# Where eleven weight conversions stand among the first chunk's products

## The chip, the core and the metric

The kernel runs on one core of a Trainium2 chip. The metric is the device time of one execution in microseconds. The time before is 731.13 us, the median of three runs (729.48 to 731.27). A difference under 0.3%, about 2.2 us, is taken as no change.

## The reference

Three stages follow each other. Stage one is attention on inputs of shape (4, 8, 768, 64), with a local window, a few global columns and a distance bias. Stage two is a feed-forward layer on the 3072 rows that come out, and it is the stage that the change touches. Stage three is a soft mixture of eight experts.

```python
def _moe_ref(x, w_in, w_out) -> np.ndarray:
    h = x @ w_in
    g = h * (1.0 / (1.0 + np.exp(-h)))
    return (g @ w_out).astype(np.float32)
```

Here x has 3072 rows of 512, w_in is 512 by 2048 and w_out 2048 by 512. NumPy draws both weights in float64, so each number reaches the chip as a pair of 32-bit words.

## The kernel before

The 3072 rows are 24 tiles of 128, in eight chunks of three. For each chunk the first layer runs 16 steps (`l1_step`, f = 0 to 15): twelve products of 128 by 384 on TensorE into one of four banks in turn (lines 502 to 504), a tanh on ScalarE (506), a gate on VectorE (508) and a split of the result into a float16 high part (ScalarE, 199) and low part (VectorE, 209). Then the second layer (`l2_part`, lines 522 to 524) sums over the same 16 blocks. The attention of the next chunk's tiles is cut into items that are dealt out after each step by `slot_end`: scores on TensorE (315 or 325), bias and maximum on VectorE (330), exponentials on ScalarE (331), splits (199, 201, 207, 209), transposes by DMA (348, 393), and products with the values (370).

Each weight is cut into eight pieces: 0 to 7 of w_in, 8 to 15 of w_out. Piece p of w_in serves first-layer steps 2p and 2p+1; piece 8+p of w_out serves second-layer blocks 2p and 2p+1. `w_ahead` loads a piece (1 MB, line 450, on SyncE's queue) into one of six staging places as soon as that is free, and `conv(p)` turns it into two float16 parts:

- line 460, ScalarE, and 462, VectorE: pick out exponent bits and mark bits;
- line 467, TensorE: two small products that gather the mark bits; after every odd piece 469, ScalarE, reads their bank before the next piece may write it;
- line 470, VectorE: join the words to a float32, over the bits that 467 read;
- line 480, ScalarE: the high part; 488, VectorE: the low part. This frees the staging place.

Pieces 8 to 15 reuse places 4, 5 and 3: piece 9 goes where piece 5 was, 10 where 3 was, then 11 where 8 was, 12 where 9 was, 13 where 10 was, 14 where 11 was, 15 where 12 was.

Pieces 0 to 4 are converted during the first chunk's attention (`START`), and the change leaves them alone. The loop of the first chunk calls `conv` for 5, 6 and 7 in front of steps 10, 12 and 14, and for 8 to 15 in front of the second layer's pairs of blocks. A scheduler then turns the program into a fixed order per engine, in which independent instructions may move forward; each engine runs its own list in order. In that list the first instructions of a conversion (460, 462) already stand early, the later ones (467 to 488) near the place of the call.

Of the kernel before, what the change touches and what calls it, by code (L numbers as in the profile page):

```python
# [45 lines left out]
def p2(e):  # L46
    return float(2.0 ** e)
# [33 lines left out]


START = [3, 9, 14, 18, 22, 99, 99, 99]
HE = 'AAAAAA'
PHE = 'AAAAAA'
PLE = 'VVVVVV'
# [13 lines left out]
def fast_kernel(tc, keepp, q_l, k_l, v_l, q_f, k_f, n_global, n_local, w_in, w_out, phi, w1, w2, shapes, pick_c, out):  # L100
# [8 lines left out]
    with ExitStack() as ctx:  # L109
# [160 lines left out]
        def split(T):  # L270
            t, u = T % TPB, T % NR
            he = HE[T] if T < len(HE) else "P"
            le = HLO[T] if T < len(HLO) else "V"
# [172 lines left out]
        def w_ahead():  # L446
            while nload[0] < 16 and holder.get(place[nload[0]]) is None and (GATE.get(nload[0]) is None or GATE[nload[0]] in done_p):
                p = nload[0]
                holder[place[p]] = p
                nc.sync.dma_start(out=ar.view(place[p], [2048], I32), in_=(w_in if p < 8 else w_out)[p % 8].bitcast(I32))  # L450
                nload[0] += 1

        def conv(p):
            assert holder[place[p]] == p
            st = ar.view(place[p], [1024, 2], I32)
            low, high = st[:, :, 0], st[:, :, 1]
            by = ar.view(place[p], [2048], I32).bitcast(U8).rearrange("p (n e) -> p n e", e=8)
            u16 = ar.view(place[p], [2048], I32).bitcast(U16).rearrange("p (n e) -> p n e", e=4)

            A.activation(out=low, in_=by[:, :, 3], func=AF.Copy, scale=1.0 / 32, bias=-0.484375)  # L460

            V.tensor_scalar(out=u16[:, :, 1], in0=u16[:, :, 3], scalar1=0xF000, scalar2=0x3000, op0=ALU.bitwise_and, op1=ALU.bitwise_xor)

            zb = u16[:, :, 1].bitcast(BF16)
            for j in range(2):
                g = 32 * (2 * (p % 2) + j)
                mm(bM[g:g + 32], wz, zb[:, 512 * j:512 * j + 512], start=True, stop=True, tile_position=(0, g))
            if p % 2 == 1:
                A.activation(out=odd16, in_=bM, func=AF.Abs, accum_out=oddp[:, p // 2:p // 2 + 1])
            V.scalar_tensor_tensor(out=low, in0=high, scalar=3, in1=low, op0=ALU.logical_shift_left, op1=ALU.bitwise_xor)  # L470
            lowf = ar.view(place[p], [1024, 2], F32)[:, :, 0]
            if p < 8:
                dst = [wih[:, z, :, 256 * p:256 * p + 256] for z in range(2)]
                src = lowf.rearrange("p (k f) -> p k f", k=4)
                e = E_WI
            else:
                dst = [woh[:, 2 * (p - 8):2 * (p - 8) + 2, z] for z in range(2)]
                src = lowf.rearrange("p (k f) -> p k f", k=2)
                e = E_WO
            A.activation(out=dst[0], in_=src, func=AF.Copy, scale=-p2(e - 128))  # L480
            if LOE[p] != "V":
                if LOE[p] == "P":
                    A.activation(out=src, in_=src, func=AF.Copy, scale=-p2(e - 128))
                else:
                    G.tensor_scalar(out=src, in0=src, scalar1=-p2(e - 128), scalar2=0.0, op0=ALU.mult, op1=ALU.add)
                G.tensor_tensor(out=dst[1], in0=src, in1=dst[0], op=ALU.subtract)
            else:
                V.scalar_tensor_tensor(out=dst[1], in0=src, scalar=-p2(e - 128), in1=dst[0], op0=ALU.mult, op1=ALU.subtract)  # L488
            holder[place[p]] = None
            w_ahead()  # L490
# [330 lines left out]
        nconv = 0  # L821
        before = START
        for i, it in enumerate(first_items()):
# [6 lines left out]
        for c in range(NCH):  # L830
            todo = items[upto[c]:upto[c + 1]] if c + 1 < NCH else []
            n = CHUNKS[c]
            nslots = 16 + 4 * n
            span = nslots - CFG["tail_slots"]
            st = {"s": 0, "d": 0}

            def slot_end():
                st["s"] += 1
                tick()
                while st["d"] < min(len(todo) * st["s"] // span, len(todo)):  # L840
                    todo[st["d"]]()
                    st["d"] += 1

            for f in range(16):
                while nconv <= min(7, f // 2):
                    conv(nconv)
                    nconv += 1
                l1_step(c, f)
                slot_end()
                if c == NCH - 1 and 1 <= f < 11:  # L850
                    w1_halves(1, False)
                elif c == NCH - 1 and f >= 14:
                    w1_halves(1)
            if c == NCH - 1:
                rows.close()
                endp = ctx.enter_context(tc.tile_pool(name="end", bufs=1))
                late["ct"] = endp.tile([128, NTILE, 128], F32R, name="ct")
                late["st"] = endp.tile([128, 2, 256], F32R, name="st")
                flat = [late["ct"][:, 3 * i:3 * i + 3].rearrange("p t c -> p (t c)") for i in range(8)]
                late["c4"] = [v.rearrange("p (t a z s) -> p t a z s", t=3, a=2, z=2) for v in flat]  # L860
                ready = first[c] // 3
                c_norm(0, 3 * ready)
                for i in range(ready):
                    c_parts(i)
                w_units([wi0 + 8192 * i for i in range(4)] + [silu0])
                per_f = 512 * n
                g_slot = [[g0 + 8192 * i for i in range(3) if min(4, -(-8192 * (i + 1) // (4 * per_f))) == q + 1] for q in range(4)]
                g_slot[3] += [g0 + 8192 * i for i in range(3) if 8192 * (i + 1) > 16 * per_f and g0 + 8192 * i not in g_slot[3]]
            if c == 0:
                for f in range(0, 16, 2):  # L870
                    conv(8 + f // 2)
                    for m in range(n):
                        l2_part(c, m, range(f, f + 2))
                    slot_end()
                    if f % 4 == 2:
                        slot_end()

                V.tensor_reduce(out=odd, in_=oddp, axis=AX.X, op=ALU.max)
                G.memset(acc, 0.0)
                G.memset(ssum, 0.0)  # L880
                G.memset(mrun[0], -3e38)
                absmax(4, wih[:, 0, 0, 0:128])
                absmax(5, woh[:, 0, 0, 0:128])
                absmax(NSMP - 1, phi16[:, :, 0], AX.XY)
                for m in range(n):
                    l2_end(c, m)
                    tick()
            elif c == NCH - 1:
                while heap:
                    tick()  # L890
                last_begin(c)
                pick = ar.view(ls0 + 512, [2, NS], F32)
                nc.sync.dma_start(out=pick, in_=pick_c.rearrange("p (s o c) -> p s o c", s=2, o=4)[:, :, 0])
                for q in range(3):
                    for f in range(4 * q, 4 * q + 4):
                        for j in range(4):
                            last_part(c, j, (f,))
                        w1_halves(1 + (f % 4 < 2))
                    w_units([wo0 + 8192 * q] + g_slot[q])
                for j in range(4):  # L900
                    last_part(c, j, range(12, 16))
                    last_end(c, j)
                    if j < 3:
                        last_turn(c, j)
                    if j in (1, 2):
                        w1_halves(1)
                w_units([home[1, 15]])
                for u in range(16):
                    home[1, u] = moved[u]
            else:  # L910
                for m in range(n):
                    for q in range(4):
                        l2_part(c, m, range(4 * q, 4 * q + 4))
                        if q == 3:
                            l2_end(c, m)
                        slot_end()
            if c < NCH - 1:
                turn[0] += n
            while st["d"] < len(todo):
                todo[st["d"]]()  # L920
                st["d"] += 1
            if c == NCH - 2:
                w_units([silu0 + 8192 * i for i in range(1, 9)])
# [457 lines left out]
```

## Time and profile before

| | |
|---|---|
| median of three runs | 731.13 us |
| profiled execution | 731.55 us, span 729.7 us |
| TensorE (PE) busy | 676.9 us, 93% |
| VectorE (DVE) busy | 502.6 us, 69% |
| ScalarE (ACT) busy | 357.4 us, 49% |
| GpSimd (POOL) busy | 251.3 us, 34% |
| mean granted TensorE clock | 0.976 of full speed |

The span is the time from the first to the last instruction of the profiled execution; 1.85 us lie around it. The averages hide stages with different limits, so the section of rows below shows stretches apart. A clock of 1.00 is 2.4 GHz, 0.50 is 1.2 GHz; a number between is a mix of the two in time.

### The profile page before, as it was taken

How to read it: one execution, taken by the hardware profiler on the slowest of the kernel's cores; microseconds unless marked ns; L12 is line 12 of the kernel's file. 1: busy time of each engine (PE TensorE's matmuls, PEld its weight loads, DVE VectorE, ACT ScalarE, POOL GpSimd, SP SyncE). 2: the span in 40 equal slices, each digit the busy share in tenths (PEclk: the TensorE clock that was granted, in tenths of full speed). 3: DMA queues.
4: the chain of work that ended last, by engine and by line, in shares of the span. 5: the costliest groups of instructions: out<-in, count | busy, mean ns of one | idle time of the engine just before them, and what ended most of it. 6: DMA issues, size and time to landing. Idle time of an engine off the chain costs nothing.

```text
span 729.7 us, 13673 instructions
## 1 busy us (share of the span) xinstructions
PE 676.9 (93%) x5175; PEld 389.8 (53%) x5175; DVE 502.6 (69%) x1189; ACT 357.4 (49%) x902; POOL 251.3 (34%) x211
## 2 busy tenths in 40 slices
PE   4779797889999999999999999999999989999993
PEld 2445353445655665466556654665566546655552
DVE  4998789986862787278727872787277248797432
ACT  5677665545531553265415532653166247575322
POOL 3110103540562558235635572356243410170000
PEclk9999898999999999999999999999999999999998
DMA  7998566844463475835654647356424793196998
GB/s 223 239 303 238 140 152 194 280 126 87 102 151 81 103 144 101 160 82 108 128 104 106 142 105 156 85 104 125 64 44 65 155 321 128 37 370 239 379 412 298
DMA packets 165257, 120.08 MB, mean 165 GB/s; under 512 B 143936, under 2 KB 150464, under 8 KB 159168
## 3 DMA queue, kind: packets, MB, share of 16 engines
q1 hardware_dynamic: 163968, 118.15, 61.1%
q10 hardware_dynamic: 1216, 0.99, 0.4%
q8 instruction: 42, 0.69, 0.4%
q14 instruction: 31, 0.25, 0.1%
HBM read 79.01 MB, written 6.29 MB: 117 GB/s over the span
## 4 chain that ended last, share of the span: by engine, by line


## 5 line engine op out<-in xcount | busy, mean ns | idle before, releaser
L201 POOL TENSOR_SCALAR arena<-arena 128x1024 f16<-128x1024 f32 (+5 forms) x115 | 121.0, 1063 | 286.3 <-ACT arena L331 110.4
L502 PE MATMUL bank<-rows,arena 128*128 128x384 f16 x512 | 169.1, 331 | 0.4 <-DVE arena L330 0.3
L503 PE MATMUL bank<-rows,arena 128*128 128x384 f16 x512 | 168.7, 330 | 0.0
L504 PE MATMUL bank<-rows,arena 128*128 128x384 f16 x512 | 168.0, 329 | 0.0
L199 ACT ACTIVATE arena<-bank 128x384 f16<-128x384 f32 (+1 forms) x153 | 77.2, 505 | 158.3 <-DVE bank L508 94.0
L331 ACT ACTIVATE arena<-arena 128x256 f32<-128x256 f32 (+1 forms) x192 | 92.4, 482 | 90.2 <-DVE arena L330 89.2
L522 PE MATMUL bank<-arena 128*128 128x512 f16 x336 | 127.9, 386 | 2.1 <-ACT arena L480 2.1
L523 PE MATMUL bank<-arena 128*128 128x512 f16 x336 | 128.4, 382 | 0.3 <-DVE arena L488 0.3
L524 PE MATMUL bank<-arena 128*128 128x512 f16 x336 | 128.1, 381 | 0.0
L209 DVE SCALAR_TENSOR_TENSOR arena<-bank,arena 128x384 f16<-128x384 f32 (+2 forms) x154 | 87.6, 570 | 31.6 <-ACT arena L199 30.6
L207 POOL TENSOR_TENSOR arena<-arena 128x1024 f16<-128x1024 f32 (+1 forms) x45 | 92.9, 2063 | 23.6 <-ACT arena L199 20.6
L330 DVE CUSTOM_DVE_ANT_0 arena<-bank,arena 128x256 f32<-128x256 f32 (+1 forms) x192 | 70.1, 394 | 33.4 <-PE bank L325 29.7
L508 DVE SCALAR_TENSOR_TENSOR bank<-arena,bank 128x384 f32<-128x384 f32 x128 | 71.0, 557 | 30.0 <-ACT arena L506 29.0
L207 DVE TENSOR_TENSOR arena<-arena 128x1024 f16<-128x1024 f32 (+2 forms) x50 | 69.3, 1386 | 10.2 <-POOL arena L201 8.5
L209 DVE SCALAR_TENSOR_TENSOR arena<-arena 128x1024 f16<-128x1024 f32 (+3 forms) x64 | 66.8, 1058 | 7.3 <-POOL arena L201 3.9
L506 ACT ACTIVATE arena<-bank 128x384 f32<-128x384 f32 x128 | 61.6, 482 | 15.5 <-PE bank L504 14.7
L504 PEld LDWEIGHTS <-arena 128*128 128x128 f16 x512 | 50.5, 99 | 34.2 <-issue 1.4
L502 PEld LDWEIGHTS <-arena 128*128 128x128 f16 x512 | 50.6, 99 | 31.7 <-issue 3.5
L503 PEld LDWEIGHTS <-arena 128*128 128x128 f16 x512 | 50.6, 99 | 29.3 <-issue 2.0
L199 ACT ACTIVATE arena<-arena 128x1024 f16<-128x1024 f32 (+1 forms) x61 | 55.4, 913 | 14.3 <-DVE arena L209 8.8
L524 PEld LDWEIGHTS <-arena 128*128 128x128 f16 x336 | 33.1, 98 | 40.2 <-issue 1.4
L522 PEld LDWEIGHTS <-arena 128*128 128x128 f16 x336 | 33.2, 99 | 38.1 <-issue 4.7
(185 smaller groups left out, 818.7 us busy)
## 6 DMA issues: line engine op xcount, KB each, us to landing
arena<-in_w_dram SPq DMA_DIRECT2D x31, 1024.0 KB, 8.8
arena<-in_k_l_dram SPq DMA_DIRECT2D x18, 512.0 KB, 4.4
arena<-in_q_l_dram SPq DMA_DIRECT2D x18, 512.0 KB, 3.9
arena<-in_w_in_dram SPq DMA_DIRECT2D x8, 1024.0 KB, 6.2
arena<-in_w_out_dram SPq DMA_DIRECT2D x8, 1024.0 KB, 5.8
arena<-in_v_l_dram SPq DMA_DIRECT2D x24, 256.0 KB, 3.1
out_dram<-arena SPq DMA_DIRECT2D x4, 768.0 KB, 8.1
arena<-in_q_f_dram SPq DMA_DIRECT2D x6, 256.0 KB, 5.3
```

The source lines that it names most:

```text
L199: A.activation(out=out, in_=in_, func=AF.Copy, scale=p2(e))
L201: G.tensor_scalar(out=out, in0=in_, scalar1=p2(e), scalar2=0.0, op0=ALU.mult, op1=ALU.add)
L207: (V if eng == "V" else G).tensor_tensor(out=out, in0=in_, in1=h, op=ALU.subtract)
L209: return V.scalar_tensor_tensor(out=out, in0=in_, scalar=p2(e), in1=h, op0=ALU.mult, op1=ALU.subtract)
L331: A.activation(out=pw, in_=pw, func=AF.Exp, scale=-1.0, bias=nmx[:, T, h:h + 1], accum_out=psum_[T % 2][:, h:h + 1])
L502: mm(hp, wh, x[:, 0, k], start=(k == 0), stop=False)
L503: mm(hp, wh, x[:, 1, k], start=False, stop=False)
L504: mm(hp, wl, x[:, 0, k], start=False, stop=(k == 3))
L508: gated.append(V.scalar_tensor_tensor(out=hp, in0=th, scalar=1.0, in1=hp, op0=ALU.add, op1=ALU.mult))
L522: mm(op, gh, woh[:, f, 0], start=(f == 0), stop=False)
L523: mm(op, gh, woh[:, f, 1], start=False, stop=False)
L524: mm(op, gl, woh[:, f, 0], start=False, stop=(f == 15))
```

## The change

A table `AHEAD` replaces the rule that set where `conv` is called in the first layer of the first chunk: pieces 5, 6, 7, 8 and 9 in front of steps 5, 8, 11, 13 and 15 (before: 5, 6, 7 in front of 10, 12, 14, and 8, 9 in front of the second layer's first two pairs). Pieces 10 to 15 are called one per pair of blocks, from the first pair on, so each comes two pairs earlier than before.

```diff
@@ -81,6 +81,7 @@
 START = [3, 9, 14, 18, 22, 99, 99, 99]
+AHEAD = [0, 0, 0, 0, 0, 5, 8, 11, 13, 15]
 HE = 'AAAAAA'
@@ -842,7 +843,7 @@
             for f in range(16):
-                while nconv <= min(7, f // 2):
+                while nconv < len(AHEAD) and AHEAD[nconv] <= f:
                     conv(nconv)
                     nconv += 1
                 l1_step(c, f)
@@ -868,7 +869,9 @@
             if c == 0:
                 for f in range(0, 16, 2):
-                    conv(8 + f // 2)
+                    if nconv < 16:
+                        conv(nconv)
+                        nconv += 1
                     for m in range(n):
                         l2_part(c, m, range(f, f + 2))
```

The new line shifts the numbers: after line 83 each line of before is one higher in the change (three higher after line 871). Loads, buffers and instructions are the same in number and kind; only their order differs.

The first place is VectorE, from the first row where its two lists part, in step 4 of the first layer. Line 462 there is piece 8's. First the list of before.

```order
L462 TENSOR_SCALAR arena<-arena 128x1024
L381 TENSOR_SCALAR arena<-arena 128x8
L382 RECIPROCAL arena<-arena 128x8
L508 SCALAR_TENSOR_TENSOR bank_73<-arena,bank_73 128x384
L207 TENSOR_TENSOR arena<-arena 128x1024
L209 SCALAR_TENSOR_TENSOR arena<-bank_73,arena 128x384
L508 SCALAR_TENSOR_TENSOR bank_74<-arena,bank_74 128x384
```

And the list of the change, where the line numbers are one higher.

```order
L463 TENSOR_SCALAR arena<-arena 128x1024
L471 SCALAR_TENSOR_TENSOR arena<-arena 128x1024
L509 SCALAR_TENSOR_TENSOR bank_73<-arena,bank_73 128x384
L382 TENSOR_SCALAR arena<-arena 128x8
L208 TENSOR_TENSOR arena<-arena 128x1024
L210 SCALAR_TENSOR_TENSOR arena<-bank_73,arena 128x384
L331 ISA arena<-bank_70,arena 128x256
L331 ISA arena 128x1
L489 SCALAR_TENSOR_TENSOR arena<-arena 128x4x256
L509 SCALAR_TENSOR_TENSOR bank_74<-arena,bank_74 128x384
```

The join (471) and the low part (489) of piece 5 now stand here; before they come after step 9's gate.

The second place is ScalarE around step 7 of the first layer. Bank 76 is step 7's, bank 73 step 8's, bank 74 step 9's. Before, line 460 here is piece 10's.

```order
L506 ACTIVATE arena<-bank_76 128x384
L331 ACTIVATE arena<-arena 128x256
L199 ACTIVATE arena<-bank_76 128x384
L331 ACTIVATE arena<-arena 128x256
L460 ACTIVATE arena<-arena 128x1024
L199 ACTIVATE arena<-arena 128x1024
L506 ACTIVATE arena<-bank_73 128x384
L506 ACTIVATE arena<-bank_74 128x384
```

In the change piece 10's 461 stands ahead of step 7's tanh, and the one shown here is piece 9's.

```order
L507 ACTIVATE arena<-bank_76 128x384
L200 ACTIVATE arena<-bank_76 128x384
L332 ACTIVATE arena<-arena 128x256 x2
L461 ACTIVATE arena<-arena 128x1024
L200 ACTIVATE arena<-arena 128x1024
L481 ACTIVATE arena<-arena 128x4x256
L507 ACTIVATE arena<-bank_73 128x384
L507 ACTIVATE arena<-bank_74 128x384
```

Piece 9's first instruction and piece 6's high part (481) have moved ahead of the tanh of steps 8 and 9; before, 480 of piece 6 comes after the tanh of step 10 and 460 of piece 9 after that of step 11.

The third place is the end of the conversions on VectorE. Before, the last three low parts (488) are those of pieces 13, 14 and 15, and bank 76 is the second chunk's first step.

```order
L488 SCALAR_TENSOR_TENSOR arena<-arena 128x2x512
L470 SCALAR_TENSOR_TENSOR arena<-arena 128x1024
L878 TENSOR_REDUCE arena<-arena 128x1
L488 SCALAR_TENSOR_TENSOR arena<-arena 128x2x512
L508 SCALAR_TENSOR_TENSOR bank_76<-arena,bank_76 128x384
L488 SCALAR_TENSOR_TENSOR arena<-arena 128x2x512
```

In the change the last two are 14's and 15's. Line 208 of 128 by 512 between them is the low part of attention's output for tile 5, the second chunk's last tile.

```order
L463 TENSOR_SCALAR arena<-arena 128x1024
L489 SCALAR_TENSOR_TENSOR arena<-arena 128x2x512
L208 TENSOR_TENSOR arena<-arena 128x512
L471 SCALAR_TENSOR_TENSOR arena<-arena 128x1024
L881 TENSOR_REDUCE arena<-arena 128x1
L331 ISA arena<-bank_71,arena 128x128
...
L208 TENSOR_TENSOR arena<-arena 64x1024
L489 SCALAR_TENSOR_TENSOR arena<-arena 128x2x512
```

The conversions no longer come in a bunch at the end; tile 5's output has come to stand close ahead of the last one.

On SyncE's queue the loads of pieces 10 and 9 come ahead of the next attention tile's three loads, where before they come behind two and three of them. From the second chunk's tenth step or so on the lists of all engines are the same again.

## Rows read from the trace of the kernel before

**Rows 1.** The page's first part: each engine's busy time over the whole span.

```profile
PE 676.9 (93%) x5175; PEld 389.8 (53%) x5175; DVE 502.6 (69%) x1189; ACT 357.4 (49%) x902; POOL 251.3 (34%) x211
```

**Rows 2.** Busy us (instructions), clock and DMA by stretch, after the first chunk.

```profile
180.00:240.00 60.00, 60.00 (x461) 34.48 (x460) 36.87 (x100) 24.23 (x73) 27.17 (x21) 1.00 0.47 105
...
600.00:660.00 60.00, 60.00 (x401) 36.03 (x400) 52.63 (x87) 40.97 (x64) 15.93 (x14) 1.00 0.52 194
```

**Rows 3.** The same view around the first chunk; the last row overlaps the others.

```profile
67.70:81.00 13.30, 13.30 (x106) 7.42 (x104) 8.85 (x22) 9.10 (x25) 0.00 (x0) 1.00 0.87 258
81.00:95.00 14.00, 10.20 (x61) 4.76 (x58) 12.59 (x23) 7.96 (x21) 2.91 (x3) 0.63 0.43 112
95.00:108.00 13.00, 12.72 (x96) 7.25 (x94) 11.39 (x20) 10.64 (x21) 1.05 (x1) 1.00 0.48 111
108.00:158.80 50.80, 41.38 (x243) 19.14 (x240) 49.56 (x80) 27.18 (x57) 21.60 (x14) 0.87 0.71 211
158.80:181.70 22.90, 21.60 (x143) 12.14 (x142) 14.45 (x38) 10.21 (x28) 3.62 (x2) 1.00 0.41 92
69.00:158.80 89.80, 76.30 (x486) 37.78 (x484) 81.20 (x143) 53.58 (x117) 25.55 (x18) 0.87 0.65 187
```

**Rows 4.** TensorE in order of time: start, us, line, shape, [idle before <-releaser].

```profile
83.17 0.61 PE L467 MATMUL bank<-arena 128*32 128x512 bf16 x2 [1.50 <-ACT arena L469]
...
89.03 0.50 PE L502 MATMUL bank<-rows,arena 128*128 128x384 f16 x1 [0.18 <-ACT arena L480]
...
115.61 0.63 PE L467 MATMUL bank<-arena 128*32 128x512 bf16 x2 [2.95 <-DVE arena L382]
...
148.93 0.61 PE L467 MATMUL bank<-arena 128*32 128x512 bf16 x2 [1.91 <-DVE arena L462]
```

**Rows 5.** VectorE's groups between 69 and 158.8: xcount | busy, mean ns | idle.

```profile
L488 DVE SCALAR_TENSOR_TENSOR arena<-arena 128x1024 f16<-128x1024 f32 x11 | 15.2, 1390 | 1.1 <-ACT arena L480 1.1
...
L462 DVE TENSOR_SCALAR arena<-arena 128x1024 uint16<-128x1024 uint16 x8 | 10.9, 1364 | 3.7 <-ACT arena L460 3.7
L207 DVE TENSOR_TENSOR arena<-arena 128x1024 f16<-128x1024 f32 x8 | 10.6, 1326 | 0.7 <-ACT arena L199 0.6
L330 DVE CUSTOM_DVE_ANT_0 arena<-bank,arena 128x256 f32<-128x256 f32 x18 | 7.1, 412 | 0.5 <-PE bank L315 0.5
L508 DVE SCALAR_TENSOR_TENSOR bank<-arena,bank 128x384 f32<-128x384 f32 x13 | 7.0, 554 | 1.5 <-ACT arena L506 1.4
...
L209 DVE SCALAR_TENSOR_TENSOR arena<-arena 128x512 f16<-128x512 f32 x4 | 3.7, 922 | 0.0
```

**Rows 6.** ScalarE in order of time: one conversion's first instruction.

```profile
79.73 1.11 ACT L460 ACTIVATE arena<-arena 128x1024 int32<-128x1024 uint8 x1 [2.03 <-DMA arena<-in_w_out_dram]
```

**Rows 7.** SyncE's queue in order of time: a transpose and a weight load.

```profile
71.36 1.93 SPq L348 DMA_TRANSPOSE arena<-arena  x1
73.33 1.02 SPq L450 DMA_DIRECT2D arena<-in_w_out_dram  x1
```

**Rows 8.** The 16 weight loads (line 450), from issue to landing.

```profile
DMA to landing us min/median/max: 4.8/6.0/8.0
```

**Rows 9.** The transposes of attention's output (line 393), from issue to landing.

```profile
DMA to landing us min/median/max: 3.0/3.2/6.8
```

**Rows 10.** VectorE in order of time: conversions' last instructions and a neighbour.

```profile
120.99 1.22 DVE L488 SCALAR_TENSOR_TENSOR arena<-arena 128x1024 f16<-128x1024 f32 x1
122.13 0.28 DVE L330 CUSTOM_DVE_ANT_0 arena<-bank,arena 128x128 f32<-128x128 f32 x1
...
135.72 3.47 DVE L488 SCALAR_TENSOR_TENSOR arena<-arena 128x1024 f16<-128x1024 f32 x2 [0.28 <-ACT arena L480]
...
157.58 1.21 DVE L488 SCALAR_TENSOR_TENSOR arena<-arena 128x1024 f16<-128x1024 f32 x1
```

**Rows 11.** GpSimd in order of time.

```profile
136.11 4.00 POOL L201 TENSOR_SCALAR arena<-arena 128x1024 f16<-128x1024 f32 x2
```

**Rows 12.** TensorE in order of time, where the two programs' orders meet again.

```profile
181.71 0.51 PE L370 MATMUL bank<-arena 128*128 128x64 f16 x12
```
## The prediction

> **What bounds the kernel now.** I read the page first: TensorE is the busiest engine by far [rows 1]. Then I read stretches: after the first chunk TensorE is busy without a break (60.00 of 60.00 us at clock 1.00, at 180 us and still at 600) [rows 2]. So a microsecond that the start loses stays lost, and one that it wins stays won, as long as the order of work behind it is the same, which it is from the second chunk's tenth step on.
>
> Around the first chunk the picture is another [rows 3]. From 67.7 to 81 TensorE is full. From 81 to 158.8 it is busy 10.20 of 14.00, 12.72 of 13.00 and 41.38 of 50.80 us: 13.5 us idle, and the granted clock falls to 0.63 and 0.87, so part of the work ran at 1.2 GHz. VectorE is the other way round. It idles 4.4 of 13.3 us while TensorE is full, 3.0 us in the next two rows together, and 1.2 of 50.8 us afterwards. It is the bound from 108 on, and not before. Over 69 to 158.8 it is busy 81.2 us and idle 8.6.
>
> The waits say why [rows 4]. From 83 on TensorE stands in front of the marks' products (467) of pieces 5 to 8, which its list has in a heap there: 1.50 us until ScalarE has read the bank (469), and step 10 at 89.03 waits for piece 5's high part (480). In the second layer it waits 2.95 and 1.91 us in front of 467 and behind VectorE. VectorE's own longest wait is for piece 10's first instruction (3.7 us in all) [rows 5], which waited 2.03 us for its load [rows 6].
>
> **The change, step by step.** The conversions lose and gain no instruction: eleven each of 470 and 488 stand between step 4 and the last low part in both lists. What changes is when they run. The second halves of pieces 5 and 6 move from after step 9 to steps 4 to 8, where VectorE has its 4.4 us of idle time. I make the sum for the moment at which the last low part ends, 158.8 us before (157.58 and 1.21 [rows 10]), and then for TensorE's row where the two orders meet, at 181.71 [rows 12].
>
> *Work put behind the last low part.* Counted from the two lists, five things of size no longer stand ahead of it: one 207 of 128 by 1024 (1.33), one 209 of 128 by 512 (0.92), two 330 of 256 (0.82) and one 508 (0.55) [rows 5], 3.6 us. Five short ones, not counted, weigh about as much as the tenth of a microsecond by which each row overlaps the next (120.99 and 1.22, but 122.13) [rows 10]. The work is not saved: it moves to where VectorE has 8.4 us to spare (14.45 of 22.90) [rows 3]. Gain 3.6.
>
> *VectorE's idle time, 8.6 us, shrinks to what is left of it.* Three remainders.
>
> First, piece 9. Its load may start when piece 5 is done. On VectorE that is 4.8 us after 69, at 73.8; SyncE's queue then takes it within 0.2 us, since the transpose ahead of it (71.36 before, 1.93 long) [rows 7] gets out at about 74. It lands 6.0 us later (4.8 to 8.0) [rows 8], at 80.0, and 460 takes 1.1 [rows 6]. Piece 9's 462 comes up on VectorE at 80.5 and would start at 81.2. Queued behind the waiting 460 on ScalarE are piece 6's high part and the tanh of steps 8 and 9, on VectorE the gates of those steps. TensorE needs them for steps 12 and 13 only, at about 87, and they are through by 86. So the price is 0.7 us, 0 to 2.7. Piece 10's load now starts at about 67.6 instead of 73.33, and its wait goes.
>
> Second, the loads of pieces 11 to 15. Each starts when a piece three places earlier is done, and ScalarE's 460 of the new piece stands ahead of the 480 of an older one. Landing, 460, 480 and the handing over need 6.0 + 1.1 + 1.1 + 0.4 = 8.6 us, 10.6 with the latest landing. VectorE's rows in between, priced by their spacing where nothing disturbs them (1.14 for a 488, from 120.99 to 122.13 [rows 10]), come to 8.8 us for piece 11, then 7.9, 10.3, 10.1 and 9.0. At 6.0 us that costs 0.7; at 8.0, 1.8 + 2.7 + 0.3 + 0.5 + 1.6 = 6.9. The channel is less full than before in the first half (0.43 to 0.48 from 81 to 108) [rows 3], so I take 2.0, near the lower end.
>
> Third, TensorE now waits for VectorE in front of the second layer for 4 to 5 us once, and its clock may fall there; then a pair of blocks at half speed can be late for VectorE's next product. Lower bound 0; upper bound the largest such wait of before, 2.95 [rows 4]. I take 1.5.
>
> Left: 0.7 + 2.0 + 1.5 = 4.2. Gain 8.6 - 4.2 = 4.4.
>
> *What is late next.* The second chunk's first products need the transposes of tile 5's output. Its low part now ends about 4.0 us of VectorE work ahead of the last conversion. The transposes land after 3.0 to 6.8 us, mostly 3.2 [rows 9], with loads beside them: TensorE may wait 0 to 2.8 us. I take 1.2 as a loss. Behind it TensorE has the same work to the meeting point as before (21.60 busy of 22.90) [rows 3].
>
> Sum: 3.6 + 4.4 - 1.2 = 6.8 us. The profiled execution took 731.55, which makes 724.75; the median of the runs is 0.42 lower, so 724.3.
>
> A rule speaks against this sum. The Trainium skill (Perfetto Trace Analysis, Identifying the Most-Contended Engine) says that a kernel gets better by improving the engine that is occupied most. By that rule VectorE, with 49.56 of 50.80 us, would have to lose work here, it loses none, and the time stays at 731. The trace agrees for 108 to 158.8 alone: 7.4 of the 8.6 idle microseconds lie ahead of it, and by the rows the sum stands.
>
> **The rivals.**
>
> *The loads set the pace* (chance 0.20). VectorE's idle time does not go but changes its cause, from the heap at step 10 to the loads. For it: three staging places in turn, landings of up to 8.0 us, and two waits for loads already in view. Against it: 8 to 10 us of cover for 8.6. With 6.9 from the loads, 2.7 from piece 9 and the 0.4 that is left of the clock, 10 us stay: 3.6 + 8.6 - 10 - 1.2 = 1.0, so 730.1; the case spans 727 to 731.5. That is also where the rule above would come out.
>
> *Piece 9 stops ScalarE and VectorE* (chance 0.06), the case on the other side. 461 of piece 9 stands ahead of two tanhs, and 463 ahead of two gates; each microsecond that the load lands after 80.5 costs one. From 88 on the gain is gone. If SyncE holds the load until 83 and it takes 8.0, it lands at 91: 10.5 us against 0.7 taken, so 734. Against it: piece 5's conversion needs only step 4, whose time the change does not touch.
>
> *VectorE gets faster too* (chance 0.14). Its instructions are slowed in places: two 488 took 3.47 us together at 135.72, against 1.22 for one at 120.99 [rows 10], while GpSimd ran 128 by 1024 [rows 11]; the eleven average 1.39 [rows 5], 1.9 us too much. If the new order parts them from GpSimd's work, and 207 and 209 gain as much again, 3.8 us come on top: 720.5. The Trainium skill (SBUF — State Buffer, Who interferes with whom) says that a VectorE instruction with two inputs in SBUF contends with a GpSimd instruction that reads SBUF. The trace agrees in this one place; by that rule the loss follows the overlap, and GpSimd's 21.60 us in that stretch have to be done in any order, which is why the chance is small.
>
> *The forecast* (chance 0.60): 724.3, within 721 to 727.
>
> **How the numbers follow.** Faster by over 0.3%, that is under 728.9: all of the forecast and of the third rival, and 0.06 of the first: 0.80. Within 0.3%: 0.12 of the first and 0.02 of the second, 0.14. Slower: 0.02 and 0.04, 0.06. The range goes from 719.5 to 729.5: it holds the forecast, the middle of the third rival and a third of the first, and leaves out some 0.2.
>
> **What would show it.** In the profile after: TensorE passes steps 8 to 13 with no wait of over 1 us in front of 467; VectorE idles about 4 us between 69 and the last low part, which ends at about 151; TensorE reaches the row of 181.71 at about 175, and is busy without a break from there. I am wrong on the loads if ScalarE's 460 of pieces 11 to 15 waits over 1 us each for its load and VectorE's idle time stays at 8; wrong on the tail if TensorE waits over 3 us for the transposes of line 393; wrong altogether if the time between 181.71's row and the end changes.

## The result, and the profile after

The changed kernel takes 724.22 us (median of 4 runs, 723.92 to 725.41) where the kernel before takes 730.45 beside it (729.48 to 731.27). The ratio is 0.9918 with a 95% interval of 0.9899 to 0.9937, a gain of 6.0 us (4.6 to 7.4). The prediction said 724.3. The profiled execution took 723.92 us, its span is 722.1. Line numbers of the changed file are one higher than before (three from 871 on): 488 is now 489, 460 is 461.

The stretches around the first chunk come first: us, then busy us (instructions) of TensorE, its weight loads, VectorE, ScalarE and GpSimd, then the granted clock, the DMA share and GB/s.

```profile
67.70:81.00 13.30, 13.30 (x100) 7.41 (x99) 12.27 (x26) 11.14 (x24) 0.00 (x0) 1.00 0.92 300
81.00:95.00 14.00, 13.03 (x104) 6.82 (x102) 13.17 (x30) 10.55 (x27) 2.50 (x3) 1.00 0.33 68
95.00:108.00 13.00, 11.40 (x79) 5.42 (x78) 12.94 (x18) 8.31 (x19) 1.78 (x2) 1.00 0.68 183
...
147.81:173.49 25.68, 22.90 (x159) 13.47 (x159) 18.12 (x48) 12.22 (x34) 7.32 (x6) 0.93 0.59 141
180.00:240.00 60.00, 60.00 (x477) 34.58 (x476) 37.08 (x92) 22.33 (x68) 28.99 (x20) 1.00 0.53 116
```

```profile
67.64:147.81 80.17, 72.98 (x472) 34.77 (x470) 76.10 (x133) 51.36 (x111) 19.47 (x15) 0.96 0.67 191
```

Against [rows 3], VectorE now works 12.27 of the 13.30 us in which TensorE is full (8.85 before), and from 81 to 95 TensorE works 13.03 us at clock 1.00 (10.20 at 0.63); from 95 to 108 it works a little less than before (11.40 for 12.72). The last row shown starts 2.35 us after the start of piece 8's first ScalarE instruction, as the 89.8 us row of [rows 3] does. From there to the last low part VectorE is busy 76.10 us and idle 4.07, where it was busy 81.2 and idle 8.6. The last low part ends at 147.81, not 158.79 (about 151 was said). From 180 to 240 TensorE has no gap, as in [rows 2]. Later on it has a few in both programs, 6.3 us in all before and 7.4 in the change, so it is not busy without a break to the end, as the prediction has it.

TensorE in order of time (start, us, line, shape, idle before and releaser), with the row of [rows 12] last:

```profile
108.57 0.70 PE L316 MATMUL bank<-arena 64*128 64x256 f32 x2 [1.68 <-DVE arena L331]
...
135.94 0.38 PE L524 MATMUL bank<-arena 128*128 128x512 f16 x1 [1.49 <-DVE arena L489]
137.15 0.61 PE L468 MATMUL bank<-arena 128*32 128x512 bf16 x2 [0.83 <-DVE arena L463]
...
162.65 0.38 PE L545 MATMUL bank<-arena 128*128 128x64 f16 x8 [2.67 <-DVE arena L548]
...
173.49 0.51 PE L371 MATMUL bank<-arena 128*128 128x64 f16 x12
```

The heap of [rows 4] is gone: the longest wait in front of the marks' products (now 468) is 0.83 us. The meeting point, where the two orders become one again, is reached at 173.49, 8.2 us earlier than in [rows 12]. But 1.36 us of that is no part of the change: piece 8's first ScalarE instruction, ahead of which both programs are alike, starts at 65.29 here and at 66.65 before. From there to the meeting point it is 108.20 against 115.06 us, 6.9 less. From it to the end it is 548.6 against 548.0; over all profiles of this document that last part takes 546.0 to 549.3.

One wait has a new cause, the 2.67 us at 162.65, at the logits. In the kernel before TensorE waits there too, for a transpose:

```profile
171.08 0.39 PE L544 MATMUL bank<-arena 128*128 128x64 f16 x8 [1.30 <-DMA arena<-arena]
```

In the change it waits for VectorE. Followed back, this begins on SyncE. VectorE, GpSimd and SyncE in order of time:

```profile
146.58 1.23 DVE L489 SCALAR_TENSOR_TENSOR arena<-arena 128x1024 f16<-128x1024 f32 x1
147.72 1.63 DVE L208 TENSOR_TENSOR arena<-arena 128x1024 f16<-128x1024 f32 x1
...
157.37 1.23 DVE L208 TENSOR_TENSOR arena<-arena 128x1024 f16<-128x1024 f32 x1 [4.00 <-POOL arena L202]
158.51 1.02 DVE L509 SCALAR_TENSOR_TENSOR bank<-arena,bank 128x384 f32<-128x384 f32 x2
```

```profile
148.37 2.00 POOL L208 TENSOR_TENSOR arena<-arena 128x512 f16<-128x512 f32 x1
156.29 1.05 POOL L202 TENSOR_SCALAR arena<-arena 128x1024 f16<-128x1024 f32 x1 [5.92 <-DMA arena<-in_k_l_dram]
```

```profile
150.40 1.23 SPq L349 DMA_TRANSPOSE arena<-arena  x1
151.72 0.53 SPq L268 DMA_DIRECT2D arena<-in_k_l_dram  x1
```

The staging buffer for k of attention tile 9 is free at 149.35, when VectorE has read tile 8's (147.72 and 1.63). Its load starts at 151.72, since a transpose stands ahead of it in SyncE's queue and waits for GpSimd's 208 (until 150.37). GpSimd can make the high part at 156.29 only, and VectorE, which stands in front of the low part for 4.00 us, has the second chunk's gates (509) and the logits' evictions (547, 548) behind it. In the kernel before the same load stands behind the same transpose, but starts at 149.78, and its low part comes up on VectorE at 159.87 only:

```profile
147.14 1.92 SPq L348 DMA_TRANSPOSE arena<-arena  x1
...
149.78 0.38 SPq L267 DMA_DIRECT2D arena<-in_k_l_dram  x1
```

From the last low part to the meeting point it is 25.68 us, against 22.92 before.

### The profile page after: what moved, and what is told of

Read it like the earlier page. It is cut to its first block, busy times and chain, and to the rows that moved or that the text cites. A ratio compares the mean times of both kernels' runs of the same rounds, so it can differ in the third digit from the quotient of the medians.

```text
span 722.1 us, 13677 instructions
## 1 busy us (share of the span) xinstructions
PE 672.4 (93%) x5175; PEld 387.1 (54%) x5175; DVE 500.4 (69%) x1189; ACT 357.3 (49%) x902; POOL 252.4 (35%) x211
## 4 chain that ended last, share of the span: by engine, by line
## 5 line engine op out<-in xcount | busy, mean ns | idle before, releaser
L202 POOL TENSOR_SCALAR arena<-arena 128x1024 f16<-128x1024 f32 (+5 forms) x115 | 118.1, 1038 | 293.4 <-ACT arena L332 112.8
```

The source lines that it names most:

```text
L202: G.tensor_scalar(out=out, in0=in_, scalar1=p2(e), scalar2=0.0, op0=ALU.mult, op1=ALU.add)
```

## The experiments

Twelve runs, in three groups of four on one chip each, beside the kernel before. The table puts their profiles on one scale. The anchor is the start of piece 8's first ScalarE instruction. "Busy" and "idle" are VectorE's between 2.35 us after the anchor (69.00 in [rows 3]) and the end of the last low part; "tail" is the time from there to the row of [rows 12].

| kernel | last low part after the anchor | busy | idle | tail | ratio to before, interval |
|---|---|---|---|---|---|
| before | 92.14 | 81.19 | 8.60 | 22.92 | 1 |
| changed | 82.52 | 76.10 | 4.07 | 25.68 | 0.9918 (0.9899 to 0.9937) |
| e1, first layer's half | 88.53 | 81.08 | 5.10 | 22.87 | 0.9936 (0.9910 to 0.9961) |
| e2, second layer's half | 88.08 | 75.72 | 10.01 | 23.61 | 0.9947 (0.9929 to 0.9965) |
| e3, k9 low on GpSimd | 83.66 | 75.77 | 5.54 | 23.04 | 0.9864 (0.9839 to 0.9889) |
| e4, the same in before | 91.67 | 82.66 | 6.66 | 22.13 | 0.9993 (0.9979 to 1.0008) |
| e5, changed again | 82.41 | 76.46 | 3.60 | 24.21 | 0.9895 (0.9874 to 0.9917) |
| e6, e3 again | 85.02 | 78.15 | 4.52 | 23.20 | 0.9868 (0.9843 to 0.9893) |
| e7, two low parts off VectorE | 92.85 | 84.47 | 6.03 | 20.32 | 0.9962 (0.9949 to 0.9976) |
| e8, one step later | 83.47 | 77.65 | 3.47 | 26.08 | 0.9924 (0.9903 to 0.9945) |
| e9, loads by ScalarE's queue | 83.39 | 76.06 | 4.98 | 22.68 | 0.9879 (0.9857 to 0.9900) |
| e10, e6 and e9 | 84.46 | 77.46 | 4.65 | 22.10 | 0.9865 (0.9835 to 0.9896) |
| e11, logits later | 84.11 | 77.48 | 4.28 | 23.64 | 0.9909 (0.9884 to 0.9934) |
| e12, steps earlier | 78.08 | 72.39 | 3.34 | 24.55 | 0.9822 (0.9797 to 0.9847) |

**e1, the first layer's half alone.**

```diff
-AHEAD = [0, 0, 0, 0, 0, 5, 8, 11, 13, 15]
+AHEAD = [0, 0, 0, 0, 0, 5, 8, 11]
```

> Only pieces 5 to 7 are brought ahead (steps 5, 8, 11); pieces 8 to 15 stand in front of their pairs of blocks as before. In VectorE's list the same work stands ahead of the last low part as in the kernel before, so the term for work put behind it is nil here, while the heap at steps 8 to 13 goes. By the prediction's sum only the idle time is left to win: 7.4 of the 8.6 idle us lie ahead of 108, about 4 us stay, so 726 (724.5 to 727.5), and the last low part ends 4 to 5 us earlier than before. Rival, the work put behind the last low part is what pays and the first half alone wins little: 729 to 730.5. Rival, VectorE as the busiest engine of the second layer eats what is won ahead of it: 730.

Measured: 726.67 us against 731.35, 4.7 us less; 726 was expected. The last low part comes 3.6 us earlier (4 to 5 was expected). VectorE's busy time ahead of it is what it was, 81.08 against 81.19, and its idle time falls from 8.60 to 5.10:

```profile
68.57:154.75 86.18, 74.13 (x488) 36.77 (x486) 81.08 (x143) 53.13 (x117) 26.45 (x18) 0.92 0.71 195
154.75:177.62 22.87, 21.61 (x143) 12.13 (x142) 14.46 (x39) 10.20 (x28) 3.62 (x2) 1.00 0.40 92
```

So the idle time is a gain by itself, and the busiest engine of the second layer does not eat it. Both rivals fall: 729 and 730 lie above the interval (724.8 to 728.5).

**e2, the second layer's half alone.**

```diff
-AHEAD = [0, 0, 0, 0, 0, 5, 8, 11, 13, 15]
+AHEAD = [0, 0, 0, 0, 0, 10, 12, 14, 15, 15]
```

> Only pieces 8 to 15 are brought ahead (8 and 9 at step 15, 10 to 15 two pairs early); pieces 5 to 7 stand at steps 10, 12 and 14 as before. In VectorE's list about 4.1 us of work (one subtraction of 64 by 1024, one of 128 by 512, two score reductions of 256 and two of 128, one gate) now stands behind the last low part, but the heap at steps 8 to 13 stays and with it VectorE's idle time there. By the prediction's sum 4.1 less 1 to 3 for the tail: 727.5 (726.5 to 729.5). Rival, the idle time of the first layer is all that counts: 730. Rival, the longer distance to the products is what pays in the second layer, whatever the first does: 724 to 725.

Measured: 727.49 us, 3.9 us less; 727.5 was expected. Here the busy time ahead of the last low part falls by 5.5 us, and the idle time grows by 1.4, since the heap stays (piece 10's first instruction waits 4.35 us on VectorE). Both rivals fall here too: 730 and 725 lie outside the interval (726.2 to 728.8). In the tail TensorE has no gap at all:

```profile
67.60:153.33 85.73, 72.51 (x455) 34.90 (x453) 75.72 (x129) 51.31 (x107) 16.49 (x13) 0.88 0.62 177
153.33:176.94 23.61, 23.61 (x176) 14.33 (x174) 17.81 (x52) 12.71 (x38) 7.95 (x7) 1.00 0.62 146
```

The two halves are the two terms of the sum, one each, though e2 puts fourteen instructions behind the last low part and the whole change ten. Alone they give 4.7 and 3.9, 8.6 us, and the whole change 6.0 (7.7 in e5). With intervals of 1.3 to 1.9 us to either side, that the whole gives less than the halves is not shown by the times. The next runs ask whether the new wait in the tail takes something back.

**e3 to e6, the new wait.** The low part of tile 9's k goes to GpSimd, in the changed kernel (e3 and e6) and in the one before (e4). The orders of TensorE and of SyncE stay as they are in e3; in e4 only one transpose and one load change places on SyncE.

```diff
-                lo("V" if le == "V" else "P", kr[:, 1, :, u], ks, E_QK, kr[:, 0, :, u])
+                lo("V" if le == "V" and T != 9 else "P", kr[:, 1, :, u], ks, E_QK, kr[:, 0, :, u])
```

> The changed kernel with one instruction on another engine: the low part of attention tile 9's k (128 by 1024) is taken by GpSimd instead of VectorE, where it waited 4.00 us for GpSimd and the load of k with the second chunk's gates and the logits queued behind it. The orders of TensorE and of SyncE stay. Theory, this wait is why the stretch from the last low part to the meeting point took 25.7 us against 22.9: TensorE's 2.67 us wait at the logits goes, and the time is 721.5 to 722.8. Rival, the stretch is longer for another reason (tanh evictions on ScalarE, the half clock, the order itself), and the wait moves to the next instruction: 724.0 within 0.5.

> The kernel before with the same instruction on GpSimd. There it stood behind the last low part (159.87, no wait in front of it) in a stretch where VectorE has 8.4 us to spare. Theory, the wait at this place is new with the change: no change, 730.4 within 0.6. Rival, fewer 128 by 1024 instructions on VectorE pay anywhere: 729 or less.

> The changed kernel once more, unedited, beside the next one on the same chip. Both theories: ratio to the kernel before 0.992, within 0.9899 to 0.994. It is the base for the next three.

> The low part of tile 9's k on GpSimd once more, beside the changed kernel on the same chip. Theory, the new wait in the tail costs 2 to 4 us: ratio to the kernel before 0.9865, 2 to 4 us under the run of the changed kernel beside it, and TensorE's wait at the logits about 1 us, not 2.7. Rival, the gain of the first look was a better chip or an earlier start: within 1 us of the changed kernel.

Measured: 722.42 and 721.71 us, where the changed kernel takes 724.22 and 723.77. By the ratios e3 and e6 are 9.9 and 9.7 us under the kernel before, the changed kernel 6.0 and 7.7, so the edit is worth 2 to 4 us (e5, at 0.9895, came out a little under the range that was expected of it). The intervals of e5 and e6 overlap, so the traces have to say the rest: the tails are 23.04 and 23.20 us, where the changed kernel has 25.68 and 24.21, that is 1.0 to 2.6 us less. The whole way from the anchor to the meeting point is not shorter in these single profiles (106.70 and 108.22 against 108.20 and 106.62), since VectorE's pace ahead of the tail, over the same list, differs by as much. In the kernel before, where the instruction stands in front of no wait, it is worth nothing that can be told (e4). TensorE's stop at the logits falls from 2.67 and 2.66 us to 0.98 and 1.61. What is left of it has moved to the low part of tile 9's v, the next instruction on VectorE that needs GpSimd. In e6:

```profile
163.00 0.69 DVE L210 SCALAR_TENSOR_TENSOR arena<-arena 128x512 f16<-128x512 f32 x1 [3.21 <-POOL arena L202]
```

**e7, two low parts taken off the busiest engine.** On top of e6:

```diff
-LOE = 'VVVVVVVVVVVVVVVV'
+LOE = 'VVVVVVVVVVVVPVPV'
```

> The kernel of the run before, and the low parts of pieces 12 and 14 made by ScalarE (a scaled copy) and GpSimd (a subtraction) instead of VectorE: two instructions of 1.2 us less on VectorE, about 2.2 us more on ScalarE and 4.3 us more on GpSimd. Theory, VectorE is now the bound of the stretch from the 67th to the 148th microsecond (76.1 busy of 80.2 us, nothing of size to wait for): 1.5 to 2.4 us faster than the run before, so 0.983 to 0.985 of the kernel before. Rival, TensorE with its half clock or ScalarE's share sets the pace, or GpSimd's subtraction slows VectorE's neighbours as much as is won: within 0.7 us of the run before, or slower.

Measured: 728.47 us, 6.8 us slower than e6, and the theory falls. GpSimd, SyncE and TensorE of e7 in order of time:

```profile
130.15 1.51 POOL L202 TENSOR_SCALAR arena<-arena 128x512 f16<-128x512 f32 x1 [8.88 <-ACT arena L332]
131.74 2.00 POOL L208 TENSOR_TENSOR arena<-arena 128x512 f16<-128x512 f32 x1
133.71 3.09 POOL L487 TENSOR_TENSOR arena<-arena 128x1024 f16<-128x1024 f32 x1
```

```profile
136.83 0.33 SPq L451 DMA_DIRECT2D arena<-in_w_out_dram  x1
```

```profile
136.85 0.38 PE L524 MATMUL bank<-arena 128*128 128x512 f16 x1 [4.63 <-POOL arena L487]
...
152.73 0.61 PE L468 MATMUL bank<-arena 128*32 128x512 bf16 x2 [3.07 <-DVE arena L463]
```

Piece 12's low part waits on GpSimd behind attention's work and then takes 3.09 us; TensorE stands for 4.63 us until it is done. Only then is piece 12's staging place free, and piece 15's load starts at 136.83 (130.16 in the changed kernel). Behind the stop the rest is late too: piece 15's first instruction comes at 146.10 (138.10), and TensorE stops for another 3.07 us. VectorE's list changed as well, though the edit does not name it: the splits of attention tile 8 (208 at 149.43) now stand ahead of piece 15's join and low part, and VectorE is busy 84.47 us ahead of the last low part, 78.15 in e6. What the stop costs and what the other order costs is not told apart, and the rival's "or slower" holds in the number. VectorE was the busiest engine of this stretch, and two instructions less on it came out 6.8 us slower, with the work taken off it behind a queue that had a wait of its own. The Trainium skill (Perfetto Trace Analysis, Identifying the Most-Contended Engine) says to optimize the engine with the highest occupancy first; in this run, taking work off that engine did not pay.

**e8 and e12, the distance.** On top of e6, which has 5, 8, 11, 13, 15:

```diff
+AHEAD = [0, 0, 0, 0, 0, 6, 9, 12, 14, 15]   # e8
+AHEAD = [0, 0, 0, 0, 0, 4, 6, 9, 12, 14]    # e12
```

> The kernel of the run with tile 9's k on GpSimd, with pieces 5 to 9 brought ahead a step less (steps 6, 9, 12, 14 and 15 for 5, 8, 11, 13 and 15). Theory, the distance matters only so far as no heap of waits forms at steps 10 to 14, and the work behind the last low part depends on the pairs of the second layer, which stay: within 1.5 us of it either way. Rival, each step of distance is worth as much as the next (five steps for 4.7 us): about 1 us slower for each step, so 1 to 2 us slower.

> Tile 9's low part of k on GpSimd, and pieces 5 to 9 brought ahead further (steps 4, 6, 9, 12 and 14). A step later cost about 4 us. Theory, what counts is that TensorE finds each conversion done and no load is awaited on VectorE; more distance meets the loads, which cannot start earlier than their staging places come free: within 1.5 us of the run with 5, 8, 11, 13, 15, or slower by the waits of pieces 9 and 10 for their loads. Rival, each step of distance is worth the same either way: 3 to 4 us faster, ratio 0.982.

Measured: e8 725.56 us, 3.9 us over e6; e12 717.76 us (0.9822), 13 us under the kernel before, the fastest of all. It is 3.4 us under e6 by the ratios, and 3.3 us under e10 of the same chip, which has the loads of e9 besides. The theory expected within 1.5 us in both, so it falls. The rival said 1 to 2 us for e8, which is too little, and 0.982 for e12, which came true. Its even price for each step isn't shown, though, for the two differences lie in different places. In e8 the last low part comes no later than in e6 (83.47 against 85.02 after the anchor), and the tail is 2.9 us longer. VectorE stands 4.87 us in front of tile 9's v, and TensorE 2.87 us at the logits (1.61 in e6), since the load of k stands behind the same transpose (rows below); and ten of the second chunk's products ran at the half clock behind that stop (0.53 us each), none in e6. Together that makes the way from the anchor to the meeting point 1.3 us longer (109.55 against 108.22). The rest of e8's 3.9 us lies outside this stretch and stays unexplained.

```profile
151.99 1.23 SPq L349 DMA_TRANSPOSE arena<-arena  x1
153.31 0.53 SPq L268 DMA_DIRECT2D arena<-in_k_l_dram  x1
```

```profile
161.91 0.69 DVE L210 SCALAR_TENSOR_TENSOR arena<-arena 128x512 f16<-128x512 f32 x1 [4.87 <-POOL arena L202]
```

In e12 the last low part comes 4 to 7 us earlier than in the runs with 5, 8, 11, 13, 15, for both reasons of the sum. Ten instructions more stand behind it (123 against 133 ahead of it), and no instruction of ScalarE or VectorE waits for the loads of pieces 10 and 9. These start 3.1 us ahead of the anchor and 4.5 behind it, against 0.9 and 8.4 behind it in the changed kernel:

```profile
68.97:144.70 75.73, 67.71 (x451) 32.63 (x449) 72.39 (x123) 50.52 (x105) 19.82 (x13) 0.95 0.69 188
144.70:169.25 24.55, 24.09 (x177) 14.46 (x176) 19.59 (x52) 11.71 (x35) 10.47 (x8) 1.00 0.58 141
```

In e12's tail TensorE works 24.09 of 24.55 us. There no transpose that waits for GpSimd stands in front of the load of tile 9's k:

```profile
145.33 1.23 SPq L394 DMA_TRANSPOSE rows<-arena  x1
146.92 0.33 SPq L268 DMA_DIRECT2D arena<-in_k_l_dram  x1
```

**e9 to e11, where the wait comes from.** In e9 (on the changed kernel) and e10 (with the edit of e6), ScalarE's queue issues two loads of tile 9:

```diff
-                nc.sync.dma_start(out=s, in_=src[T])
+                (nc.scalar if T == 9 and src is not q_l else nc.sync).dma_start(out=s, in_=src[T])
```

and in e11 the changed kernel's logits come two slots later:

```diff
-            at(6 if c == 0 else CFG["lag_l"], lambda: logits(c, m))
+            at(8 if c == 0 else CFG["lag_l"], lambda: logits(c, m))
```

> The changed kernel with the loads of tile 9's k and v issued by ScalarE's queue instead of SyncE's, where k's stood at 151.72 behind a transpose that waits for GpSimd, though its buffer was free at 149.35. All compute stays on its engine, TensorE's order stays. Theory, the new wait comes from this place in SyncE's queue: the load starts about 2.3 us earlier, VectorE's 4.0 us at the low part shrink to 1 to 2, TensorE's 2.7 us at the logits to under 1; 1.5 to 2.7 us under the changed kernel, ratio 0.987 to 0.989. Rival, the load is as late through traffic or GpSimd as through the queue: ratio 0.9906 as the changed kernel.

> The run before together with tile 9's low part of k on GpSimd. Theory, nothing of the tail's new wait is left on VectorE but the low part of v, and the stretch from the last low part to the meeting point is back at about 23 us: ratio 0.985 to 0.987. Rival, either edit alone takes all that there is: no faster than the better of the two alone (0.987).

> The changed kernel with the first chunk's logits put into the lists two slots later (eight after the layer's end, not six). Theory, VectorE's 4 us at tile 9's k hold back the second chunk's gates as much as the logits, so TensorE's wait moves to the next bank that it needs, and at most 1 us is won: ratio 0.989 to 0.992. Rival, it is the bank of the logits alone: TensorE's 2.7 us go, ratio 0.987.

Measured: e9 722.42 us, 8.8 us under the kernel before by the ratio (6.0 and 7.7 for the changed one); the rival's 0.9906 lies outside its interval. Tile 8's low part, ahead of which the buffer isn't free, ends at 151.14 there, and the load starts at 151.17, not 2.4 us later:

```profile
151.17 0.34 ACTq L268 DMA_DIRECT2D arena<-in_k_l_dram  x1
```

```profile
149.51 1.63 DVE L208 TENSOR_TENSOR arena<-arena 128x1024 f16<-128x1024 f32 x1
...
155.94 1.23 DVE L208 TENSOR_TENSOR arena<-arena 128x1024 f16<-128x1024 f32 x1 [0.78 <-POOL arena L202]
```

VectorE waits 0.78 us, not 4.00, TensorE has no wait over 0.7 us in the tail, and the tail is 22.68 us long. So the place in SyncE's queue makes the wait. Both edits together (e10, 721.09 us, 0.9865) win no more than the one on GpSimd (0.9864 and 0.9868), as the rival has it; but the ratio lies in the theory's range as well, and the tail is 22.10 us, so the two are not told apart. In e11 TensorE's stop is still 2.10 us, at 168.53, and the time, 724.45 us, that of the changed kernel, as the theory said; the rival's 0.987 is out. The wait did not move to the next bank, though: it is still at the logits, whose evictions stand behind gates that VectorE's wait (4.08 us here) had held up. So putting the logits two slots later does not take it away.

## Why the prediction was right

**The sum, 6.8 us.** The time came out at 724.22 for 724.3. From the anchor to the meeting point the profile shows 6.9 us less, and e5 8.4.

**Work put behind the last low part, 3.6.** Right in kind, too small in size, and one of its five instructions is miscounted. In the two traces 143 and 133 VectorE instructions stand in this stretch. The ten that went are one 209 of 128 by 512, one 209 of 128 by 384, two 330 of 256, one 508 and five short ones. The prediction has a 207 of 128 by 1024 (1.33 us) where the 209 of 128 by 384 (0.55) belongs; eight such 207 stand ahead of the last low part in both. At the durations of before the five are 2.8 us and all ten 3.65, so the 3.6 comes near what the list gives by luck. VectorE's busy time falls by 5.1. Added up instruction by instruction it falls by 4.2, the ten and 0.5 of pace; the other 0.9 is overlap, since a row that need not wait overlaps its neighbour ([rows 10]) and fewer wait now. e2, which has this term and not the other, loses 5.5 us. The pace differs between executions: seven profiles (changed, e3, e5, e6, e9, e10, e11) have the same VectorE list up to the last low part, and are busy 75.77 to 78.15 us over it.

**Idle time down to 4.2, a gain of 4.4.** In the profiled execution 4.07 is left, and over the seven 3.60 to 5.54, 4.5 in the mean. The kernel before has 8.60 and, in e4, 6.66, so the gain is nearer to 3.1. e1 has this term alone: 3.5. Of the three remainders two were sized well. Piece 9's load costs VectorE 1.03 us (0.7 said). TensorE's lag costs 1.25 (1.5 said), the way that was said: TensorE waited for VectorE (1.68 us at 108.57, where 4 to 5 was said), products behind that ran at the half clock, 0.43 us apart instead of 0.22, and VectorE's join 471 waited for them:

```profile
113.00 0.63 PE L524 MATMUL bank<-arena 128*128 128x512 f16 x1
```

```profile
117.16 1.72 DVE L471 SCALAR_TENSOR_TENSOR arena<-arena 128x1024 int32<-128x1024 int32 x1 [1.25 <-PE bank L468]
```

The loads of pieces 11 to 15 cost VectorE nothing that the rows show (2.0 said). Of the five only piece 11's is waited for, 2.42 us on ScalarE, whose next instruction then waited another 0.80 us for VectorE:

```profile
105.78 1.16 ACT L461 ACTIVATE arena<-arena 128x1024 int32<-128x1024 uint8 x1 [2.42 <-DMA arena<-in_w_out_dram]
```

In place of these 2.0 us stand two waits that no remainder names, 0.78 us for TensorE's scores (at 94.53) and 0.63 for ScalarE (at 119.93 and 120.96), which had waited for the same late products. So 4.07 for 4.2 is partly luck.

The two terms' errors, 1.5 up and 1.3 down, cancel: over the seven profiles the last low part ends 83.7 us after the anchor, over before and e4 91.9, and 8.2 us lie between, where 8.0 was said.

**What is late next, a loss of 1.2.** This step named the wrong wait. The transposes of tile 5's output were to make TensorE wait; the second chunk's first products have no wait in the profile. What was late was the load of tile 9's k, 2.4 us behind in SyncE's queue. The tail grew by 2.8 us in the profiled execution and by 1.3 in e5. TensorE's idle time in it went from 1.30 us to 2.78 and 2.84; the rest of the 2.8 is products at the half clock in the one execution. The runs put the price of the late load at 2 to 4 us (e3, e6) or 1 to 3 (e9). The size was near, the cause was not seen. The prediction counted the loads of weights past which pieces move, and not that attention's load of k keeps its place behind a transpose in SyncE's list while VectorE's last low part comes 11 us earlier. That transpose even starts later than before (150.40 for 147.14): the exponentials that it goes back to over GpSimd's split stand behind piece 15's high part on ScalarE now (332 at 145.88), where before they stood ahead of the last two pieces' first instructions (331 at 142.43).

**The rivals.** That the loads set the pace is out: 4.07 us of idle time stay, not 10, and most have other causes. That piece 9 stops ScalarE and VectorE is out: 0.65 and 1.03 us. That VectorE gets faster is not shown: its 489 take 1.35 us in the mean (1.39 in [rows 5]), but its 471 take 1.37 (1.24 before). That VectorE would have to lose work for the time to fall is out: it runs 1189 instructions in both programs, as in [rows 1]. One reading of [rows 5] was off, without weight in the sum: of the 3.7 us of waits in front of 462, 3.07 are piece 10's and 0.66 piece 8's, ahead of the stretch. The loads were not made later or slower by themselves in any run, so their price from there on stays open.

## What to carry to other kernels

Moving work earlier on a bounding engine has two gains that can be counted apart, in its list (what now stands behind its last due instruction) and in its idle time (what was waited for); the two halves of this change, run alone, show one each. Then follow the transfers that were timed by the old pace: a load that stands in an in-order queue behind a transpose that waits for a slower engine starts late however early its buffer is free, and here that took back 1 to 4 us of some 10, by which run one asks. An engine being the busiest in a stretch does not say that work taken from it pays; look first at what is queued on the engine that would take it.

## What the runs showed of the hardware

The low part of a piece, one VectorE instruction on 128 by 1024, took 1.21 us in e12 (at 143.49) with GpSimd idle, and 3.00 us in e7 while GpSimd ran 208 (2.12 us) beside it. The Trainium skill (SBUF — State Buffer, Who interferes with whom) says that a VectorE instruction with two inputs in SBUF contends with a GpSimd instruction that reads SBUF; these two rows agree:

```profile
156.46 3.00 DVE L489 SCALAR_TENSOR_TENSOR arena<-arena 128x1024 f16<-128x1024 f32 x1
```

```profile
156.25 2.12 POOL L208 TENSOR_TENSOR arena<-arena 128x1024 f16<-128x1024 f32 x1
```

The same stop of TensorE, 2.67 us in the changed kernel and 2.66 in e5, was followed in the one by nine products at the half clock (0.52 us each, 0.32 apart, from 163.81 on), in the other by none (0.33, 0.16 apart). That is about 1.5 us between two executions of the same program, and the tails of 25.68 and 24.21 differ by as much:

```profile
163.81 0.52 PE L503 MATMUL bank<-rows,arena 128*128 128x384 f16 x1
164.13 0.52 PE L504 MATMUL bank<-rows,arena 128*128 128x384 f16 x1
```

```profile
165.48 0.33 PE L503 MATMUL bank<-rows,arena 128*128 128x384 f16 x1
165.64 0.33 PE L504 MATMUL bank<-rows,arena 128*128 128x384 f16 x1
```
